# Issuing the load of token tile 1 from ScalarE's DMA queue instead of second in SyncE's

## The chip, the cores and the metric

The kernel runs on one core of a Trainium2 chip. The metric is the device time of one execution in microseconds (us). "Tile n" is the block of 128 tokens with number n. Times inside an execution count from the start of the profiled span.

## The reference, cut to what matters

```python
xn = layernorm(x)                        # x: 2048 tokens x 1024, bf16
s  = attention(xn, wqkv, wo)             # 32 heads of 32
g  = silu(mlp(layernorm(xn), w1, b1, w2, b2))
return x + s * g
```

Nothing of the attention can start before tiles are loaded and normalised, so the first loads of x and the first statistics are the kernel's start-up.

## The kernel before

The program is written as a list of operations. A small scheduler records each one with its engine and what it reads and writes, works out the semaphore waits, and uses an estimated clock to decide in which order filler work is queued. The loads come first, all on SyncE's queue:

```python
def load_x(tb):
    op("sync", lambda e: e.dma_start(xst[:, tb * D:(tb + 1) * D], x2[tb * 128:(tb + 1) * 128, :]),
       w=[("xst", tb)], dma=f"x{tb % 8}", c=256)
# [...]
load_x(0)
load_x(1)
load_x(2)
load_wq(0, (1,))     # 512 KB of weights
load_x(3)
load_wq(0, (0,))
load_x(4)
load_x(5)
load_wq(0, (2,))
for tb in range(6, NT):
    load_x(tb)
# [...]
```

VectorE takes the statistics of tile 0, ScalarE those of tile 1 (two passes over the tile), and GpSimd does the power for the reciprocal standard deviation:

```python
def norm_pair(p):
    if p == 0:
        stat(0)            # VectorE, L324, L328
        rstd(0, 1)         # VectorE L338, GpSimd L340
        stat_scalar(1)     # ScalarE L715, L716, L717, then GpSimd L718, L719
        xnorm(0)           # VectorE L359
        bn_half(2, 0)      # VectorE L324
        xnorm(1)           # VectorE L359: needs tile 1's factor
        bn_half(2, 1)
        bn_merge(2)
        # [...]
```

TensorE transposes the normalised tiles (L386), makes K and Q (L689) and V (L705), and then scores (L872). ScalarE's exp (L884) and TensorE's matmuls fill the rest of the run.

The softmax here doesn't subtract the row's maximum and nothing guards it: scores larger than these inputs give would overflow.

## Time and profile before

| Kernel before | us |
|---|---|
| device time, median of 3 runs | 1090.31 (1090.11 to 1090.38) |
| span of the profiled run | 1088.8 |
| tile 0 lets VectorE start | 3.35 |
| tile 1 lets ScalarE start | 4.03 |
| normalisation of tile 1 (VectorE) starts | 7.41 |
| first exp starts | 14.79 |

The profile's instruction rows read: start, duration, engine, line and operation, output<-input, shapes, count; in brackets the idle time before and who ended it. A load's own row is only its issue (SPq, ACTq). When it landed is seen from the row of the engine that waited for it, or from the DMA row of the chain. The rows of the start-up are shown in the prediction.

### The profile page before, as it was taken

Reading aid. Unit: us, or ns where it says so; the run is one execution under the profiler, and the core shown is the slowest. Engines: PE = TensorE matmul, PEld = TensorE weight load, DVE = VectorE, ACT = ScalarE, POOL = GpSimd, SP = SyncE. Lnnn points to the kernel's source line nnn. Section 1 sums busy time; section 2 is a strip of 40 time slices with the busy share of each in tenths; the row PEclk is TensorE's granted clock in tenths of the full one; section 3 lists DMA queues with packets and bytes.
Section 4 is the critical chain, followed back from the end, with each engine's and each line's share of the span. In section 5 each row is a group of like instructions: output and inputs, shape, how many; then the busy total and the mean of one; then the engine's idle time right before and its main releaser. Section 6 shows DMA issues by size and latency. Waiting matters only on the chain.

```text
span 1088.8 us, 61842 instructions
## 1 busy us (share of the span) xinstructions
PE 1078.1 (99%) x29167; PEld 701.4 (64%) x29167; DVE 627.6 (58%) x1396; ACT 1043.9 (96%) x1197; POOL 22.4 (2%) x69
## 2 busy tenths in 40 slices
PE   9999999999999999999999999999999999999998
PEld 6766666666666666666666666666666666666665
DVE  8487843477732576642377743378733387635556
ACT  7899998999999999999999999999999999999993
POOL 4400000000000000000000000000000000000000
PEclk9999999999999999999999999999999999999999
DMA  7944365413464214355333274423253343684534
GB/s 242 185 127 139 119 177 138 125 52 110 119 154 123 68 59 128 101 104 148 90 100 100 73 155 124 120 81 109 81 135 115 91 123 106 192 206 105 109 92 123
DMA packets 209336, 131.92 MB, mean 121 GB/s; under 512 B 52538, under 2 KB 200250, under 8 KB 209082
## 3 DMA queue, kind: packets, MB, share of 16 engines
q1 hardware_dynamic: 209082, 127.97, 43.4%
q8 instruction: 228, 3.74, 1.5%
q14 instruction: 26, 0.21, 0.1%
HBM read 104.87 MB, written 12.06 MB: 107 GB/s over the span
## 4 chain that ended last, share of the span: by engine, by line
PE 57%; ACT 41%; DVE 1%; DMA 0%; issue 0%; POOL 0%; SPq 0%
ACT P L884 37%; PE ps L395 34%; PE ps L872 9%; PE ps L901 6%; PE ps L904 6%; ACT u L565 4%; PE ps L705 1%; PE ps L689 1%; DVE stats L324 0%; DMA OT<-in_A_x_dram 0%; ACT thz L609 0%; DVE wq L669 0%; DVE hT L359 0%; ACT hT L716 0%; DVE wq L671 0%
## 5 line engine op out<-in xcount | busy, mean ns | idle before, releaser
L884 ACT ACTIVATE P<-ps 128x1024 bf16<-128x1024 f32 x1024 | 968.9, 1084 | 10.3 <-PE ps L872 5.4
L901 PE MATMUL ps<-P,VP 128*32 128x256 bf16 x4096 | 257.0, 273 | 0.5 <-issue 0.5
L904 PE MATMUL ps<-P,ones 128*32 128x256 bf16 x4096 | 256.8, 273 | 0.0
L395 PE MATMUL ps<-hT,war 128*32 128x352 bf16 (+1 forms) x5376 | 225.8, 309 | 0.1
L395 PE MATMUL ps<-yTc,war 128*32 128x352 bf16 (+1 forms) x5376 | 225.3, 309 | 0.0
L872 PE MATMUL ps<-QT,KT 32*128 32x256 bf16 x4096 | 203.7, 273 | 3.4 <-issue 0.6
L395 PEld LDWEIGHTS ps<-hT,war 128*32 128x32 bf16 x5376 | 128.0, 96 | 74.4 <-issue 25.8
L395 PEld LDWEIGHTS ps<-yTc,war 128*32 128x32 bf16 x5376 | 127.3, 96 | 74.2 <-DVE xb L548 18.9
L872 PEld LDWEIGHTS ps<-QT,KT 32*128 32x128 bf16 x4096 | 60.8, 92 | 115.6 <-issue 61.9
L605 DVE TENSOR_SCALAR zh<-ps,b2h 128x352 f32<-128x352 f32 (+1 forms) x48 | 27.5, 572 | 183.4 <-PE ps L395 183.4
L548 DVE TENSOR_SCALAR xb<-ps,b1T 128x352 f32<-128x352 f32 (+1 forms) x168 | 96.2, 573 | 48.7 <-PE ps L395 44.2
L571 DVE SCALAR_TENSOR_TENSOR hT<-u,xb 128x352 bf16<-128x352 f32 (+1 forms) x168 | 84.4, 509 | 68.3 <-ACT u L565 68.2
L901 PEld LDWEIGHTS ps<-P,VP 128*32 128x32 bf16 x4096 | 109.8, 97 | 21.3 <-issue 2.1
L904 PEld LDWEIGHTS ps<-P,ones 128*32 128x32 bf16 x4096 | 109.7, 97 | 18.6
L395 PE MATMUL ps<-xnT,wq 128*32 128x352 bf16 (+1 forms) x2688 | 112.7, 309 | 0.0
L395 PEld LDWEIGHTS ps<-xnT,wq 128*32 128x32 bf16 x2688 | 63.7, 96 | 37.2 <-DVE xb L548 8.9
L558 DVE SCALAR_TENSOR_TENSOR u<-u,xb 128x352 f32<-128x352 f32 (+1 forms) x168 | 82.5, 509 | 1.9
L554 DVE TENSOR_TENSOR u<-xb 128x352 f32<-128x352 f32 (+1 forms) x168 | 82.5, 507 | 0.7
L565 ACT ACTIVATE u<-u 128x704 f32<-128x704 f32 (+1 forms) x84 | 71.8, 859 | 0.0
L395 PE MATMUL ps<-xnT,OT 128*32 128x352 bf16 (+2 forms) x1568 | 62.9, 306 | 0.2 <-DVE wq L669 0.2
L395 PE MATMUL ps<-wq,xnT 128*32 128x256 bf16 x1536 | 50.8, 274 | 0.0
L395 PEld LDWEIGHTS ps<-xnT,OT 128*32 128x32 bf16 x1568 | 37.9, 96 | 19.7 <-DVE wq L669 7.7
(61 smaller groups left out, 477.3 us busy)
## 6 DMA issues: line engine op xcount, KB each, us to landing
war<-in_B_w_dram SPq DMA_DIRECT2D x336, 256.0 KB, 3.4
wq<-in_A_wqkv_dram SPq DMA_DIRECT2D x36, 128.0 KB, 2.3
OT<-in_A_x_dram SPq DMA_DIRECT2D x16, 256.0 KB, 5.7
xnT<-in_A_x_dram SPq DMA_DIRECT2D x16, 256.0 KB, 2.9
out_dram<-wq SPq DMA_DIRECT2D x15, 256.0 KB, 2.0
y_scratch<-OT SPq DMA_DIRECT2D x14, 256.0 KB, 2.4
gT_scratch<-gst SPq DMA_DIRECT2D x32, 88.0 KB, 3.3
xnT<-in_A_wo_dram SPq DMA_DIRECT2D x8, 256.0 KB, 4.0
```

The costliest lines, as they stand in the source:

```text
L395: ins = e.matmul(outs(j), lhsT=lhs(j), rhs=rhs, start=start, stop=stop, tile_position=(0, 32 * j), skip_group_check=True)
L548: x0 = op("vector", lambda e: e.tensor_scalar(xb[:, 0:n], bank(bk, 0, n), b1T[:, f:f + 1], None, op0=ALU.add), r=[("b", bk), "b1"], w=[kx] ...
L554: x = op("vector", lambda e: e.tensor_tensor(ub[:, 0:n], xb[:, 0:n], xb[:, 0:n], op=ALU.mult), r=[kx], w=[ku], c=151 + 1.042 * n)
L558: x = op("vector", lambda e: e.scalar_tensor_tensor(ub[:, 0:n], ub[:, 0:n], 1.0 / 0.044715, xb[:, 0:n], op0=ALU.add, op1=ALU.mult), r=[kx, ...
L565: x = op("scalar", lambda e: e.activation(ut[:, :, 0:n], ut[:, :, 0:n], ACT.Tanh, scale=0.7978845608028654 * 0.044715), r=kus, w=kus, c=48 ...
L571: op("vector", lambda e: e.scalar_tensor_tensor(hT[:, fq, 0:n], ut[:, i, 0:n], 1.0, xq[:, 0:n], op0=ALU.add, op1=ALU.mult), r=[kus[i], kq] ...
L605: x0 = op("vector", lambda e: e.tensor_scalar(zh[:, 0:n], bank(bk, 0, n), 0.25, b2h[:, nb:nb + 1], op0=ALU.mult, op1=ALU.add), r=[("b", bk ...
L689: ins = e.matmul(bank(bk, off, off + w), lhsT=wq[:, which, dc, 0:128], rhs=xnT[:, dc, t0 + lo:t0 + lo + w], start=dc == 0, stop=dc == DC - ...
L872: ins = e.matmul(bank(bks[j], kh * 256, (kh + 1) * 256), lhsT=KT[i2][32 * j:32 * j + 32, k0:k0 + 128], rhs=QT[i2][32 * j:32 * j + 32, qb * ...
L884: op("scalar", lambda e, p=p, sl=sl: e.activation(pb[:, 2 * p:2 * p + 2, :, :].rearrange("p a b q -> p (a b q)"), ps[:, sl * 1024:(sl + 1) ...
L901: e.matmul(bankq(ACC, j, 0, QW), lhsT=VP[vp][:, kb, vo + 32 * j:vo + 32 * j + 32], rhs=pb[:, j, kh, :], start=first, stop=False, tile_posi ...
L904: ins = e.matmul(bankq(ACC, j, QW, 2 * QW), lhsT=ones[:, 0:32], rhs=pb[:, j, kh, :], start=False, stop=last, tile_position=(0, 32 * j), sk ...
```

## The change

The intent is to save one issue slot on SyncE: tile 1 is issued at the same moment as tile 0, by an engine that waits for it anyway.

```diff
         def load_x(tb):
-            op("sync", lambda e: e.dma_start(xst[:, tb * D:(tb + 1) * D], x2[tb * 128:(tb + 1) * 128, :]),
+            op("scalar" if tb == 1 else "sync", lambda e: e.dma_start(xst[:, tb * D:(tb + 1) * D], x2[tb * 128:(tb + 1) * 128, :]),
                w=[("xst", tb)], dma=f"x{tb % 8}", c=256)
```

## The prediction

> **What bounds the kernel now.** I read the page from the top: busy shares, the chain that ended last, then the chain in order of time for the first 18 us, because the change touches one of the first instructions. After that came the instructions of VectorE and ScalarE in order of time, and the windows by stage, which give the DMA rate.
>
> The page's busy shares and its chain by engine:
>
> ```profile
> PE 1078.1 (99%) x29167; PEld 701.4 (64%) x29167; DVE 627.6 (58%) x1396; ACT 1043.9 (96%) x1197; POOL 22.4 (2%) x69
> PE 57%; ACT 41%; DVE 1%; DMA 0%; issue 0%; POOL 0%; SPq 0%
> ```
>
> TensorE and ScalarE share the bound. No wait on a DMA shows in the body at all. Only the prologue can feel this change, and it is small: VectorE and DMA together are about 1% of the chain.
>
> The same chain in order of time, at the start (start, duration, what):
>
> ```profile
> 0.72 0.39 SPq L275
> 1.11 0.06 issue
> 1.17 2.83 DMA OT<-in_A_x_dram
> 4.00 0.02 issue
> 4.03 1.16 ACT hT L715 x2
> 5.18 0.03 issue
> 5.21 1.24 ACT hT L716 x2
> 6.45 0.10 ACT mv L717
> 6.55 0.19 POOL lnp L718
> 6.73 0.07 issue
> 6.81 0.58 POOL lnp L719
> 7.38 0.03 issue
> 7.41 0.55 DVE hT L359
> ```
>
> This is exactly the transfer that is moved. Tile 1 is issued at 1.17, one issue slot behind tile 0, and lands at 4.00. ScalarE's statistics of it, GpSimd's power and VectorE's normalisation at 7.41 hang on it. From there the chain goes down VectorE's queue to the transposes of tiles 4 and 5 at 16.53, after which TensorE runs almost without a gap. So whatever this landing gains or loses can reach the end one for one, and hardly more.
>
> How much room stands beside it, from VectorE's and then ScalarE's instructions in order of time (in brackets: idle time before, and who ended it):
>
> ```profile
> 3.35 1.29 DVE L324 BATCH_NORM_STATS2 stats<-OT 128x6 f32<-128x512 bf16 x2 [1.99 <-DMA OT<-in_A_x_dram]
> 6.21 0.69 DVE L324 BATCH_NORM_STATS2 stats<-OT 128x6 f32<-128x512 bf16 x1
> 7.41 0.55 DVE L359 TENSOR_SCALAR hT<-OT,mv,lnp 128x1024 bf16<-128x1024 bf16 x1 [0.51 <-POOL lnp L719]
> ...
> 0.72 1.28 ACT L715 ACT_TABLE_LOAD   x1 [0.72 <-PEq L1044]
> 4.03 1.06 ACT L715 ACTIVATE hT<-OT 128x1024 bf16<-128x1024 bf16 x1 [2.02 <-DMA OT<-in_A_x_dram]
> ```
>
> Tile 0 lets VectorE start at 3.35. VectorE's own queue, fed by tile 0, arrives at 6.90 (6.21 + 0.69) and then stands idle 0.51 us until tile 1's factor comes. So tile 0's side has 0.51 us of slack against tile 1's side; a gain on tile 1 is worth at most 0.51, and only if tile 0 does not get later.
>
> The DMA rate in stages (last two columns: share of the DMA engines, GB/s):
>
> ```profile
> 2.50:2.75 0.25, 0.25 (x2) 0.11 (x1) 0.00 (x0) 0.00 (x0) 0.00 (x0) 1.00 1.02 385
> 2.75:3.00 0.25, 0.25 (x2) 0.04 (x1) 0.00 (x0) 0.00 (x0) 0.00 (x0) 1.00 1.10 385
> 12.00:14.00 2.00, 2.00 (x24) 1.81 (x22) 1.97 (x5) 1.57 (x2) 1.52 (x5) 1.00 1.05 405
> ```
>
> While tiles 0 and 1 arrive the engines already move 385 GB/s, near the best they reach anywhere (405).
>
> **What the Trainium skill says.** "DMA: Bandwidth & Descriptors", section "Issuing engines are not separate DMA queues": transfers started by different engines run on the same 16 DMA engines and interleave, and a second issuer only saves issue time. The trace agrees so far as it can: tiles 0 and 1, issued 0.45 us apart (0.72 and 1.17), land 0.67 us apart (the shortest issue-to-landing time of these loads is 2.6 us, 0.72 + 2.6 = 3.3, against 4.00), and 262,144 B in 0.67 us is 391 GB/s, the full rate. Tile 1 follows tile 0 at the pace of the bytes, not of the issues. Same page, "Queues, rings and completion order": an engine takes turns between the queues that have work, a packet at a time. No run here shows this yet; before, all data is on one queue. "Perfetto Trace Analysis", section "DMA Instruction — HWDGE (DVE, Sync)": descriptor generation is one shared block that an issuing sequencer locks, so two issues at 0.72 may not run side by side; also not shown yet. "ScalarE: Activation LUTs", "What ACT_TABLE_LOAD costs": 1283 ns for the load; the trace has 1.28 us.
>
> **The change part by part.**
>
> 1. SyncE loses one issue: tile 2 and everything after it is issued about 0.45 to 0.47 us earlier (0.39 us of issue plus the gap). That is worth nothing later on: from 6 us to 16 us the queue is the limit (359 to 405 GB/s in the windows), and the bytes are the same. Tile 2 is not needed until 6.21 and tile 3 until 8.72.
>
> 2. ScalarE gains one issue as its first instruction, at 0.72. I estimate it at SyncE's 0.39 us, or about twice that, 0.8 us, if it waits for the shared block. The table load belongs to the first ACTIVATE (it carries that line), so it should follow the issue: it ends at 2.4 to 2.8 instead of 2.0. ScalarE then waits for tile 1 anyway until about 4. Cost on the path: 0, since there are 2.02 us of idle time there.
>
> 3. Tile 1's issue moves from 1.17 to 0.72 (or about 1.1 behind the lock). If issue were what it waits for, this would give 0.45 us. It is not: tile 0 holds the engines until its own bytes are through. At 391 GB/s the two tiles together take 1.34 us of all 16 engines, whichever goes first, so the later of the two still lands at about 4.0.
>
> 4. The order can become a mixture. If the engines alternate between the two queues, tile 0 is slowed by up to 0.67 us (3.33 to 4.0). 0.51 of it is slack, so 0.16 us reaches the normalisation of tile 1. If ScalarE's issue is the later one by 0.39 us, tile 0 has 0.28 us left and becomes 0.28 us later, which is inside the slack; but then tile 1 shares the engines with tile 2, which is now right behind tile 0, and finishes its second half at half rate: it has had 0.28 us worth by then, and the 0.39 us that are left take 0.78, so tile 1 lands 0.39 us later, 4.4.
>
> 5. The program's build-time clock decides the order of all other work. It charges each load 870 ns of transfer against 480 ns of issue, so in it the transfers set all landing times and they stay what they were. ScalarE's clock starts at 480 ns instead of 0, long before its first input. I expect the same instruction order on every other engine, so no change in the body.
>
> Sum: 0 (steps 1, 2, 5) plus step 3 and 4, from 0 to +0.4 us, and I take +0.1 us: 1090.31 + 0.1 = 1090.4 us.
>
> **The rivals.** *Issue-bound*: tile 1 really lands 0.45 us earlier. For it: before 2.5 us the engines are not full (106 GB/s from 1.5 to 2.0, 197 and 229 in the next two quarters), and a second queue could fill those holes. Against it: the 0.67 us between the landings. Were tile 1 at 3.55, VectorE's idle 0.51 would shrink to 0.06; TensorE's idle time before the transposes of tile 3 is 0.37, so about 0.4 us would come out at the end: 1089.9. *Mixture*: both tiles late, as in step 4: 1090.5 to 1090.7. *Table load first*: were the table load put ahead of the issue, tile 1 would be issued at 2.0 instead of 1.17, and everything on SyncE's queue would be ahead of it or alternate with it; it would land 0.8 us later or more: 1091.1 or above. Against it: the load's line is the first ACTIVATE's. *A cold second queue*: ScalarE's first transfer may need longer to start than the 1.03 us after which I see the first data of tile 0 (issued 0.72, moving at 1.75); nothing before shows it; each 0.1 us costs 0.1.
>
> **Range and chances.** The three runs before lie within 0.27 us. The outcomes above lie between -0.4 and +0.8; I give about 20% to a gain of 0.2 to 0.5, 45% to a change within 0.15, 30% to a loss of 0.15 to 0.6, and 5% to more. That makes 1089.9 to 1091.0 for 8 in 10. Two per cent is 21.8 us; all the waiting in the prologue that depends on this load is under 4 us, so within 2% is all but sure: faster 0.005, same 0.99, slower 0.005.
>
> **What would show it.** In the changed kernel: ScalarE's issue stands at 0.72 ahead of the table load (step 2); its first ACTIVATE starts at 4.0 to 4.4 (steps 3 and 4; at 3.6 the issue-bound rival is right; after 4.7 the table load or a cold queue); VectorE's first statistics at 3.35 to 4.0 (step 4); the normalisation of tile 1 at 7.4 to 7.8; TensorE's transposes of tiles 4 and 5 move from 16.53 by the same amount; from 6 us on the DMA rate is as before (step 1). It would be wrong if the order of instructions in the body changed, or if the shift at 16.53 did not reach the end one for one.

## The result

The changed kernel took 1090.68 us, median of 5 runs (1090.19 to 1091.53). The kernel before, with two more runs, had a median of 1090.11 (1088.63 to 1090.38). The ratio was 1.0007, 95% interval 0.9993 to 1.002. The single comparison does not tell a loss from nothing. The trace of the start-up does.

The page of the changed kernel, chain by engine (in the kernel before it was PE 57% and ACT 41%; VectorE and DMA are about 1% in both):

```profile
PE 55%; ACT 44%; DVE 1%; DMA 0%; issue 0%; POOL 0%
```

The chain of the changed kernel in order of time, at the start (start, duration, what):

```profile
0.73 3.93 DMA OT<-in_A_x_dram
4.66 0.02 issue
4.68 1.16 ACT hT L715 x2
...
8.18 0.55 DVE hT L359
```

In this profile the chain is the same up to the normalisation of tile 1, link by link, but tile 1 now takes 3.93 us from issue to landing instead of 2.83. It was issued 0.44 us earlier and landed 0.66 us later. The normalisation of tile 1 moved from 7.41 to 8.18.

Instructions of the changed kernel in order of time (ScalarE's issue, its table load, VectorE's and ScalarE's first work, the work of VectorE on tile 2):

```profile
0.73 0.40 ACTq L275 DMA_DIRECT2D OT<-in_A_x_dram  x1
1.16 1.28 ACT L715 ACT_TABLE_LOAD   x1 [1.16 <-PEq L1044]
4.50 1.29 DVE L324 BATCH_NORM_STATS2 stats<-OT 128x6 f32<-128x512 bf16 x2 [3.15 <-DMA OT<-in_A_x_dram]
4.68 1.06 ACT L715 ACTIVATE hT<-OT 128x1024 bf16<-128x1024 bf16 x1 [2.24 <-DMA OT<-in_A_x_dram]
7.37 0.69 DVE L324 BATCH_NORM_STATS2 stats<-OT 128x6 f32<-128x512 bf16 x1
```

Tile 0, which was not touched, is the bigger loser: VectorE starts on it at 4.50 instead of 3.35. The two tiles now land within 0.2 us of each other. VectorE's own queue gets to 8.06 (7.37 + 0.69), so nearly all of the 0.51 us in which it stood idle before tile 1's normalisation is gone. ScalarE's issue cost nothing by itself: 0.40 us, and its table load was done at 2.44, long before the tile came.

The windows by stage, two stages of each kernel (last column GB/s). Before:

```profile
1.75:2.50 0.75, 0.75 (x3) 0.30 (x2) 0.00 (x0) 0.26 (x1) 0.00 (x0) 1.00 0.87 210
2.50:3.50 1.00, 1.00 (x4) 0.31 (x3) 0.15 (x1) 0.00 (x0) 0.00 (x0) 1.00 0.97 356
```

After:

```profile
1.75:2.50 0.75, 0.75 (x3) 0.30 (x2) 0.00 (x0) 0.69 (x1) 0.00 (x0) 1.00 0.60 167
2.50:3.50 1.00, 1.00 (x4) 0.32 (x3) 0.00 (x0) 0.00 (x0) 0.00 (x0) 1.00 0.99 326
```

The engines did not move more with two queues feeding them, but a little less: 0.75 x 167 + 326 = 451 KB by 3.5 us, against 0.75 x 210 + 356 = 514 KB. At 391 GB/s the difference is 0.16 us. It is not a chance of this pair: from 1.5 to 3.5 us the three profiles of the kernel before moved 258, 241 and 245 GB/s and those of the changed kernel 225, 223 and 200, which in the mean is again 0.16 us.

One more row of the changed kernel matters, TensorE's weight loads for the first V:

```profile
13.31 1.64 PEld L705 LDWEIGHTS ps<-wq,xnT 128*128 128x128 bf16 x16 [0.21 <-DMA wq<-in_A_wqkv_dram]
```

Here V waited for the third block of weights as well. In the kernel before it started at 12.35 without that wait. Whether the second queue did that too is one of the questions below.

### The profile page after: what moved, and what is told of

Same layout as the page of the kernel before. It is cut to its first block, busy times and chain, and to the rows that moved or that the text cites. A ratio compares the mean times of both kernels' runs of the same rounds, so it can differ in the third digit from the quotient of the medians.

```text
span 1089.1 us, 61842 instructions
## 1 busy us (share of the span) xinstructions
PE 1077.0 (99%) x29167; PEld 701.0 (64%) x29167; DVE 627.2 (58%) x1396; ACT 1043.8 (96%) x1197; POOL 22.6 (2%) x69
## 3 DMA queue, kind: packets, MB, share of 16 engines
q8 instruction: 228, 3.74, 1.5%
## 4 chain that ended last, share of the span: by engine, by line
PE 55%; ACT 44%; DVE 1%; DMA 0%; issue 0%; POOL 0%
ACT P L884 40%; PE ps L395 32%; PE ps L872 9%; PE ps L901 6%; PE ps L904 5%; ACT u L565 4%; PE ps L705 1%; PE ps L689 1%; DMA OT<-in_A_x_dram 0%; ACT thz L609 0%; DVE stats L324 0%; PE ps L386 0%; DVE wq L669 0%; ACT hT L716 0%; DVE wq L671 0%
```

## The experiments

**Theory (mixture).** Two queues that start together are served in turn by the same DMA engines, so both tiles are done only when both are through. **Rivals.** *Chance*: one of the 16 parts of a load was slow in the one profile. *The moved load itself*: ScalarE's queue or its issue is slow to start. *A second queue as such* costs something, whatever it carries. *The table load* belongs ahead of the issue and delays it.

All kernels gave correct results. The instruction order on TensorE, VectorE, ScalarE and GpSimd of each edited kernel was compared with that of the kernel before; apart from the added and moved instructions it is the same. The repeats labelled again carry one comment line on top, so their line numbers are one higher. The diffs below are shortened (...); in hold_tile2, tile2_on_act, both_on_act, act_after_table and offset_only they are against the changed kernel, in the others against the kernel before.

| Kernel | VectorE starts (tile 0) | ScalarE starts (tile 1) | tile 1 normalised from | first exp | ratio to before, 95% interval |
|---|---|---|---|---|---|
| before | 3.35 | 4.03 | 7.41 | 14.79 | |
| again_before | 3.53 | 4.19 | 7.57 | 14.97 | 0.9999 (0.9987 to 1.0012) |
| third_before | 3.43 | 4.16 | 7.54 | 15.06 | 1.0001 (0.9988 to 1.0013) |
| after | 4.50 | 4.68 | 8.18 | 15.77 | 1.0007 (0.9993 to 1.002) |
| again_after | 4.98 | 4.80 | 8.44 | 15.80 | 1.0009 (0.9995 to 1.0022) |
| third_after | 4.75 | 4.57 | 8.21 | 15.57 | 1.0006 (0.9992 to 1.0019) |
| hold_tile2 | 4.18 | 4.34 | 7.86 | 16.64 | 1.0013 (1.0001 to 1.0026) |
| swap_on_sync | 4.12 | 3.44 | 7.59 | 14.95 | 1.0005 (0.9993 to 1.0018) |
| tile2_on_act | 4.53 | 5.28 | 8.67 | 16.04 | 1.0009 (0.9996 to 1.0023) |
| bias_on_act | 3.53 | 4.16 | 7.62 | 15.56 | 1.0005 (0.9991 to 1.0019) |
| both_on_act | 3.37 | 3.97 | 7.43 | 17.42 | 1.0016 (1.0001 to 1.0031) |
| split_tile0 | 2.98, second half 4.42 | 3.93 | 7.51 | 15.84 | 1.0017 (1.0004 to 1.003) |
| act_after_table | 3.74 | 4.36 | 7.82 | 15.19 | 1.0008 (0.9995 to 1.0022) |
| offset_only | 3.86 | 4.51 | 7.89 | 15.26 | 1.0007 (0.9995 to 1.002) |

The whole times cannot carry a verdict on a few tenths of a microsecond: single runs of the kernel before lay between 1088.55 and 1092.01. Only the intervals of hold_tile2, both_on_act and split_tile0 lie wholly above 1. The start-up in the profiles can, because the normalisation of tile 1 and the first exp repeat within 0.3 us.

### again_before and third_before: the kernel before, unchanged

> The kernel before, unchanged, to see how much of its prologue and of its whole time repeats. Mixture theory (the two queues share the DMA engines, so the second queue is what made tiles 0 and 1 late): tile 0 lands at 3.3 to 3.4, tile 1 at 3.9 to 4.1, the normalisation of tile 1 starts at 7.3 to 7.5, the transposes of tile 4 at 16.4 to 16.7, as in the first profile. Chance theory (one of the 16 DMA engines was slow in the one profile of the changed kernel, whatever the queues): such a slow engine turns up in this kernel's second profile about as often, and tile 0 may land at 4 or later. Time against the kernel before: ratio 1.000, and a spread of single runs of 0.5 us or more, since the first two sets of runs of the same program lay at 1088.6 to 1090.4.

> The kernel before a third time. What is open: in several profiles one of the 16 parts of a load lands 1 to 2 us after the others (in the first profile of the changed kernel the third part of the first weights landed at 13.3, and V had to wait for it), and it is not clear whether the second queue causes that or chance. Mixture theory, with the late part as chance: tile 0 at 3.3 to 3.6, tile 1 at 3.9 to 4.2, normalisation of tile 1 at 7.3 to 7.6; the last part of the third weights may land anywhere from 11.9 to 13.3. Second queue as the cause of the late part: here it lands at 11.9 to 12.5 again, as in the first two. Whole time: ratio to the kernel before 0.999 to 1.001.

Measured: tile 0 lets VectorE start at 3.53 and 3.43, tile 1 ScalarE at 4.19 and 4.16, the normalisation of tile 1 starts at 7.57 and 7.54. The start-up of the first profile repeats to 0.2 us. No profile of this kernel shows tile 0 after 3.6, so chance alone does not explain 4.50. The body, on the other hand, does not repeat. The longest single waits of TensorE's weight loads for the scores, between 340 and 560 us (total us, times, longest us), in the first profile:

```profile
PEld ps L872 <- issue: 10.7, 48, 0.8
```

and in third_before:

```profile
PEld ps L872 <- issue: 10.3, 49, 0.2
```

The first profile has single stalls of 0.7 to 0.8 us, with nothing visible that TensorE waited for; the third has none there. From 345 to 644 us the first profile loses 1.65 us on the third. Stalls of 0.3 to 1.5 us turn up at other places in other profiles, of both kernels and of the edited ones. Stalls of this size help to spread the whole time; what causes them is open. The last of the 16 parts of the third weights, which V needs, landed at 12.48 and 12.56 here and at 11.92 in the first profile. At 12.56 it is a little past the 12.5 that the second queue as the cause allowed.

### again_after and third_after: the changed kernel, unchanged

> The changed kernel, unchanged. Mixture theory: tile 0 lands at 4.2 to 4.6 and tile 1 at 4.4 to 4.8 again, the normalisation of tile 1 starts 0.6 to 0.9 us later than before, the first exp 0.8 to 1.0 us later, and the whole is 0.3 to 0.9 us slower (ratio 1.0003 to 1.0008). Chance theory: tile 0 lands at 3.4 to 4.0 and tile 1 at about 4.0, the normalisation of tile 1 at 7.4 to 7.6, and the whole is within 0.2 us of the kernel before.

> The changed kernel a third time. Mixture theory: tile 0 at 4.2 to 5.0, tile 1 at 4.5 to 4.9, normalisation of tile 1 at 8.1 to 8.5, first exp 0.8 to 1.0 us later than in the kernel before; ratio 1.0003 to 1.0012. If the second queue also causes the late part: the last part of the third weights lands after 12.7; as chance: anywhere from 11.9.

Measured: both land late again, in all three profiles. Over the three pairs of profiles the means are (differences taken before rounding): tile 0 from 3.44 to 4.74 (+1.31), tile 1 from 4.13 to 4.68 (+0.56), the normalisation of tile 1 from 7.51 to 8.28 (+0.77), the first exp from 14.94 to 15.71 (+0.77). The chance rival falls. The last part of the third weights landed at 12.73 and 12.48, which the second queue as its cause (after 12.7) does not fit in third_after. In again_after the wait has changed sides; VectorE in order of time:

```profile
7.84 0.69 DVE L325 BATCH_NORM_STATS2 stats<-OT 128x6 f32<-128x512 bf16 x1
8.44 0.53 DVE L360 TENSOR_SCALAR hT<-OT,mv,lnp 128x1024 bf16<-128x1024 bf16 x1
```

There is no bracket before the normalisation: VectorE comes straight from its own queue, which tile 0 had held up, and no longer waits for tile 1's factor. The same is so in third_after. In these two profiles the chain that ended last starts at tile 0's landing (4.95 and 4.73) and runs down VectorE's queue; only in the first profile does it start at tile 1's. So the change mostly turned a wait for tile 1 into a late tile 0.

The end gets about all of it. At the 100th exp, at 134 us, the three profiles of the changed kernel are on average 0.78 us behind the three of the kernel before (mean offsets to third_before of +0.72 and -0.06). After that the body's stalls blur it in a single profile. Pooled, 15 runs of the changed kernel have a mean of 1090.74 us and 42 runs of the kernel before one of 1089.96. The difference is 0.78 us with a standard error of 0.20 (from standard deviations of 0.54 and 0.90). The runs come from several chips, so this supports the trace rather than standing alone.

### tile2_on_act: another tile on ScalarE's queue

```diff
-            op("scalar" if tb == 1 else "sync", ...
+            op("scalar" if tb == 2 else "sync", ...
```

> Tile 1 stays second on SyncE; tile 2, which nobody needs before 6.2 us, goes to ScalarE's queue instead. Mixture theory: it takes every second turn of the engines from the start, so tile 0 lands at 4.0 to 4.9 and tile 1 even later than with the change, at 4.5 to 5.5, although tile 1 was not touched; the normalisation of tile 1 starts 0.7 to 1.5 us later than before and the first exp 0.8 us later or more. Rival, a property of the moved load itself (its issue, its own start-up on ScalarE's queue): tiles 0 and 1 land at 3.3 to 3.5 and 4.0 to 4.2 as before, and the prologue is as before.

Measured, VectorE and ScalarE in order of time:

```profile
4.53 1.29 DVE L324 BATCH_NORM_STATS2 stats<-OT 128x6 f32<-128x512 bf16 x2 [3.17 <-DMA OT<-in_A_x_dram]
5.28 1.06 ACT L715 ACTIVATE hT<-OT 128x1024 bf16<-128x1024 bf16 x1 [2.84 <-DMA OT<-in_A_x_dram]
8.67 0.55 DVE L359 TENSOR_SCALAR hT<-OT,mv,lnp 128x1024 bf16<-128x1024 bf16 x1 [0.59 <-POOL lnp L719]
```

Tiles 0 and 1 stand where they stood before the change, on the same queue in the same order, and are 1.1 to 1.2 us later than before's means (3.44 and 4.13), because a tile that nobody needed yet shared the engines with them. The mixture theory holds. The rival that the moved load itself is slow falls.

### both_on_act: ScalarE's queue by itself

```diff
-            op("scalar" if tb == 1 else "sync", ...
+            xo[tb] = op("scalar" if tb < 2 else "sync", ...
-               w=[("xst", tb)], dma=f"x{tb % 8}", c=256)
+               w=[("xst", tb)], dma=f"x{tb % 8}", c=256, after=[xo[0]] if tb == 2 else ())
```

> Tiles 0 and 1 both from ScalarE's queue, one behind the other, and SyncE starts with tile 2 once tile 0 has landed: ScalarE's queue alone, nothing mixed until then. Mixture theory: tile 0 lands at 3.3 to 3.5 and tile 1 at 4.0 to 4.3, as from SyncE; in between the landings 0.65 to 0.75. Rival, ScalarE's queue is slower to start (0.36 us in the first profile of the changed kernel): tile 0 at 3.7 or later, tile 1 at 4.4 or later. The rest comes later than before in either case (tile 2 after 5.5), so the whole is slower by 0.5 to 1.5 us in the prologue.

Measured, VectorE and ScalarE in order of time:

```profile
3.37 1.29 DVE L324 BATCH_NORM_STATS2 stats<-OT 128x6 f32<-128x512 bf16 x2 [2.01 <-DMA OT<-in_A_x_dram]
3.97 1.06 ACT L715 ACTIVATE hT<-OT 128x1024 bf16<-128x1024 bf16 x1 [1.08 <-DMA OT<-in_A_x_dram]
```

Alone, ScalarE's queue is as quick as SyncE's: 3.37 and 3.97, 0.60 apart. No cold queue. The first exp came 2.5 us later than in before's three profiles, since everything behind was held back on purpose; the expectation of 0.5 to 1.5 us for that was too low.

### bias_on_act: a second queue with almost nothing in it

```diff
-            op("sync", lambda e: e.dma_start(brow[0:FB, :], ...
+            op("scalar", lambda e: e.dma_start(brow[0:FB, :], ...
-            op("sync", lambda e: e.dma_start(brow[FB:FB + DC, :], ...
+            op("scalar", lambda e: e.dma_start(brow[FB:FB + DC, :], ...
```

> All tiles stay on SyncE; only the two small bias loads (9 KB together) are issued from ScalarE at the start. The second queue is opened, but has next to nothing to share. Mixture theory: tile 0 lands at 3.3 to 3.6 and tile 1 at 4.0 to 4.3, the normalisation of tile 1 at 7.3 to 7.6. Rival, opening a second queue costs by itself (the engines' start, or the shared descriptor generator): tile 0 lands after 3.8 and tile 1 after 4.4.

Measured, VectorE's normalisation of tile 1 and TensorE's first V:

```profile
7.62 0.55 DVE L359 TENSOR_SCALAR hT<-OT,mv,lnp 128x1024 bf16<-128x1024 bf16 x1 [0.34 <-POOL lnp L719]
13.11 1.92 PE L705 MATMUL ps<-wq,xnT 128*128 128x256 bf16 x16 [0.39 <-DMA wq<-in_A_wqkv_dram]
```

The tiles came as before (3.53 and 4.16), so an open second queue is not what delays them; its bytes are. But the first exp still came at 15.56, because V waited for the weights, the same wait as in the first profile of the changed kernel. In the trace's semaphore records the 16 parts of that load landed between 11.3 and 13.1. It is a second way for the start-up to get late, and it appears without a tile on ScalarE's queue.

### hold_tile2: tiles 0 and 1 alone on the engines

```diff
-               w=[("xst", tb)], dma=f"x{tb % 8}", c=256)
+               w=[("xst", tb)], dma=f"x{tb % 8}", c=256, after=[xo[0]] if tb == 2 else ())
```

(with tile 1 on ScalarE, and `xo[tb]` keeping each load)

> The changed kernel, but SyncE holds tile 2 and all behind it back until tile 0 has landed, so tiles 0 and 1 have the DMA engines to themselves. Mixture theory with tile 2 as the third sharer: tile 1 lands at about 4.0 and tile 0 at 3.7 to 4.0 (two tiles need 1.34 us of engine time from 1.75, plus 0.6 to 0.9 until the semaphore), the normalisation of tile 1 at 7.4 to 7.6; but tile 2 is issued only at about 4, lands after 6, and the weights come later, which costs TensorE. Rival, slow start of ScalarE's queue (its first data came 0.36 us after SyncE's): tile 1 lands at 4.3 or later even with nothing behind it.

Measured, VectorE in order of time:

```profile
4.18 1.29 DVE L324 BATCH_NORM_STATS2 stats<-OT 128x6 f32<-128x512 bf16 x2 [2.82 <-DMA OT<-in_A_x_dram]
```

Tile 1 came at 4.34. Without a third load behind them both are earlier than in the changed kernel (4.50 to 4.98 and 4.57 to 4.80), but not at the 3.7 to 4.0 and 4.0 that I expected of the mixture alone: tile 0 is 0.74 us later than before's mean of 3.44, tile 1 0.21 later. Sharing between the two tiles gives more than half of tile 0's loss. What lies behind them gives the rest or part of it; one profile cannot fix its share. The weights came later, as expected, and the first exp at 16.64.

### swap_on_sync: tile 1 first, on one queue

```diff
-        load_x(0)
         load_x(1)
+        load_x(0)
```

> The kernel before with tile 1 issued first and tile 0 second, both on SyncE: undoes the second queue, keeps the idea that tile 1 should come earlier. One queue in order: tile 1 lands at 3.3, tile 0 at 4.0. VectorE's work on tile 0 then starts at 4.0, the normalisation of tile 1 is held by VectorE's own queue at about 7.55, 0.15 us later than before; the transposes of tile 4 at 16.6 to 16.8. If tile 1's landing alone set the prologue, the normalisation of tile 1 would start at 6.75 instead. Time: within 0.3 us of the kernel before.

Measured, VectorE in order of time:

```profile
7.59 0.53 DVE L359 TENSOR_SCALAR hT<-OT,mv,lnp 128x1024 bf16<-128x1024 bf16 x1
```

One queue keeps order here: tile 1 came at 3.44 and tile 0 at 4.12. The normalisation of tile 1 then waited for VectorE's own queue (no bracket), at 7.59, 0.08 after before's mean. The slack of about 0.5 us on tile 0's side is real, and giving tile 1 the first place uses it up for nothing.

### split_tile0: a version that might have beaten both

```diff
-        load_x(0)
-        load_x(1)
+        load_x(0, 0, 512); load_x(1)
+        load_x(0, 512, D)
```

(load_x takes a range of columns; the statistics of tile 0 wait for each half by itself)

> A version that might beat both: one queue, in the order first half of tile 0's columns, tile 1, second half of tile 0. The mixture is chosen by order instead of by two queues. In a queue served in order: first half lands at about 3.0, tile 1 at 3.7, second half at 4.0. VectorE's first statistics start at 3.0, its second at 4.0, done at 4.7 as before; tile 1's factor comes 0.3 us earlier, the normalisation of tile 1 at 7.0 to 7.2, the first exp 0.2 to 0.4 us earlier than before. If half rows (1 KB pieces instead of 2 KB) move more slowly, the second half lands after 4.2 and the gain is gone. Whole time: 0.3 us less, below what the runs resolve (single runs of the kernel before spread over 3 us).

Measured, VectorE in order of time:

```profile
2.98 0.69 DVE L324 BATCH_NORM_STATS2 stats<-OT 128x6 f32<-128x512 bf16 x1 [1.62 <-DMA OT<-in_A_x_dram]
4.42 0.69 DVE L324 BATCH_NORM_STATS2 stats<-OT 128x6 f32<-128x512 bf16 x1 [0.75 <-DMA OT<-in_A_x_dram]
```

A miss. The first half came at 2.98 as expected, but tile 1 at 3.93 instead of 3.7 and the second half at 4.42 instead of 4.0. The normalisation of tile 1 starts at 7.51, the mean of before, so nothing was gained there, and V again waited for the weights (its first matmul at 13.39, 0.41 us of idle time ended by that load). No version here beats the kernel before.

### act_after_table: my rival of the table load

```diff
-        load_x(0)
-        load_x(1)
+        load_x(0); op("vector", lambda e: e.memset(lnp[:, 3, 0:1], 0.0), w=["pre"], c=100.0)
+        op("scalar", lambda e: e.activation(lnp[:, 3, 1:2], lnp[:, 3, 0:1], ACT.Tanh), ...); load_x(1)
```

> The changed kernel with a tiny activation ahead of ScalarE's issue, so that the table load comes first and tile 1 is issued at about 2.2 to 2.4: my rival of the table load, made real. Mixture theory: tile 0 has the engines almost to itself and lands at 3.3 to 3.7, as before; tile 1 then takes every second turn beside tile 2 and the first weights, needs two times 0.67 us from about 3.3, and lands at 5.0 to 5.6; the normalisation of tile 1 at 8.4 to 9.0, the first exp 1.0 to 1.6 us later than before. If instead the early issue is what delayed tile 1 (both queues starting cold at once), tile 1 lands within 2 us of its issue, at 4.4 or earlier.

Measured, ScalarE in order of time:

```profile
0.72 1.28 ACT L299 ACT_TABLE_LOAD   x1 [0.72 <-PEq L1044]
...
0.89 0.38 ACTq L275 DMA_DIRECT2D OT<-in_A_x_dram  x1
```

The run did not do what it was built for. The issue stood behind the table load and the activation in ScalarE's queue, and went out at 0.89 while the table load ran until 2.00. The issue does not wait for the work ahead of it to finish, only for the semaphore that VectorE's fill set, so the table load was never a rival. The 0.17 us that the fill cost had an effect of its own: tile 0 at 3.74 and tile 1 at 4.36, 0.62 apart, so no longer in step. Both came earlier than in all three profiles of the changed kernel, although tile 1 was issued later. That asked for the next run.

### offset_only: ScalarE's issue 0.16 us behind SyncE's

```diff
-        load_x(0)
-        load_x(1)
+        load_x(0); pre = op("vector", lambda e: e.memset(lnp[:, 3, 0:1], 0.0), w=["pre"], c=100.0)
+        load_x(1, [pre])
```

> The changed kernel, but ScalarE's issue waits for a one-column fill by VectorE, so that it starts about 0.15 us after SyncE's; the table load stays behind the issue. In the run with the tiny activation the issue came at 0.89 (it did not wait for the table load, as I had thought), and the engines then served tile 0, tile 1 and tile 2 one after the other. If the 0.17 us of offset did that (two issues that start together have their rows dealt out in turn, two that start apart do not): tile 0 lands at 3.3 to 3.8, tile 1 at 4.0 to 4.4, 0.6 to 0.7 apart, and the normalisation of tile 1 starts at 7.4 to 7.9. If the order was chance, or came from the activation or the table load: the tiles alternate again, both land between 4.2 and 5.0 and within 0.2 of each other, and the normalisation of tile 1 starts at 8.1 to 8.5. Whole time within what the runs resolve in either case.

Measured, in order of time:

```profile
0.88 0.38 ACTq L275 DMA_DIRECT2D OT<-in_A_x_dram  x1
...
3.86 1.29 DVE L324 BATCH_NORM_STATS2 stats<-OT 128x6 f32<-128x512 bf16 x2 [2.50 <-DMA OT<-in_A_x_dram]
7.89 0.55 DVE L359 TENSOR_SCALAR hT<-OT,mv,lnp 128x1024 bf16<-128x1024 bf16 x1 [0.48 <-POOL lnp L719]
```

Tile 1 came at 4.51, 0.65 after tile 0 and just outside the 4.0 to 4.4 that I gave. The two tiles are served one after the other again, without an activation and with the table load in its usual place. The offset did it. The trace's DMA records say the same: each of the 16 parts of a load ends with a 4-byte write. With both issues within 0.01 us of each other (changed kernel, three profiles) the earliest such write of tile 0 stands at 3.36 to 3.50, beside the earliest of tile 1 at 3.36 to 3.49; the rows were dealt out in turn. With 0.16 to 0.17 us between the issues, tile 0's stand at 2.62 to 3.49 and tile 1's at 3.42 to 4.14. That the engines take rows in the order in which the issues hand them over is my inference; it fits, and no run shows the mechanism.

Even so both tiles are about 0.2 to 0.4 us later than before in these two runs (the normalisation at 7.82 and 7.89, against a mean of 7.51). So rows dealt out in turn are not the whole cause: 0.31 to 0.38 of the changed kernel's 0.77 is left without them. tile2_on_act has such a remainder too: sharing alone would put its tiles at about 4.13 and 4.80 (my estimate: tile 0 at tile 1's old time, tile 1 one tile's 0.67 later), and they came at 4.53 and 5.28. Part of it is the rate. From 1.5 to 3.5 us the engines moved 200 to 225 GB/s in all six profiles with a tile on each queue and more loads right behind (the changed kernel's three, tile2_on_act and these two), against 241 to 261 in the three of the kernel before, swap_on_sync, bias_on_act, both_on_act and hold_tile2. For this run, 220 against before's mean of 248 is worth 0.14 us at 391 GB/s. One queue is no guarantee: split_tile0, with half rows, moved 215. Why the rate is lower, and the rest, stay unexplained.

## Why the prediction was right or wrong, point by point

The measured 1090.68 lies in the range of 1089.9 to 1091.0, and within 2% was right. That the number fits is partly luck: two errors cancel (see the sum). The working beneath it was right in most of its structure and wrong in two sizes, and with them in the path.

- **The path.** Right in that the start-up's shift reaches the end about one for one: +0.77 at the normalisation, +0.77 at the first exp, +0.78 at 134 us, and +0.78 in the pooled runs. Right only in one profile of three in that tile 1's landing sets it: in the other two the chain comes from tile 0 over VectorE's own queue. That no wait on a DMA shows in the body was not quite so either: two weight loads of TensorE waited for one after 16 us (at 24.64 and 29.15), 0.5 us together, too little to matter here.
- **Step 1, SyncE's earlier issues are worth nothing.** Right. Tile 2 was issued at 1.17 instead of 1.64, and neither the tiles' statistics nor the first V came earlier in any profile of the changed kernel.
- **Step 2, ScalarE's issue is free.** Right, at the lower figure: 0.39 to 0.40 us in all three profiles, with no sign in the issue's row of waiting for the shared block that the Trainium skill describes in "Perfetto Trace Analysis", section "DMA Instruction — HWDGE (DVE, Sync)", though both engines issued within 0.01 us. In the DMA records one queue's first row came 0.10 to 0.36 us after the other's; whether the block does that is open.
- **Step 3, the later of the two tiles still lands at about 4.0.** This step failed. The later of the two came at 4.68, 4.98 and 4.75, mean 4.80, against a mean of 4.13 in the three profiles of before: 0.68 us for which the sum had 0. Two parts of it show. The engines moved less while both queues started (about 0.16 us), and the 16 parts spread out: in the DMA records the earliest closing write of tile 1 hardly moved (means 3.47 before, 3.44 after), the latest went from 3.76 to 4.27. Why some parts lag is open; holding tile 2 back brought the later of the two to 4.34.
- **Step 4, the mixture.** Right in kind, wrong in size for tile 0: I gave it at most +0.67, it lost 1.31, because what the pair lost in step 3 comes on top of the sharing (0.69, from 3.44 to tile 1's old 4.13). So of the slack of 0.51 next to nothing is left. The expected half rate beside tile 2 is not what delays tile 1 by itself: with both issues offset, and tile 2 right behind, the tiles kept their order.
- **Step 5, the same instruction order.** Right, checked on every engine. (In the traces at most 48 of TensorE's 29167 matmul records stand in another order inside short groups; between unchanged copies up to 24 do.)
- **The sum.** +0.1 us was too small; the start-up lost 0.77, and the pooled runs 0.78 with a standard error of 0.20. A loss of that size was in the class to which I gave 5%. The number still fell in the range because the base was off the other way: the three runs gave 1090.31, the 42 runs have a mean of 1089.96. With the true shift on my base, 1090.31 + 0.77 = 1091.08, it would have been just outside.
- **The signs.** ScalarE's issue stood ahead of the table load, as I said, and the transposes of tiles 4 and 5 moved from 16.53 to 17.31 in the first profile. But tile 1 came at 4.57 to 4.80 and not at 4.0 to 4.4, tile 0 at 4.50 to 4.98 and not at 3.35 to 4.0, the normalisation at 8.18 to 8.44 and not at 7.4 to 7.8. Read by my list, a tile 1 after 4.7 (4.80 in again_after) would have pointed to the table load or a cold queue, and it was neither.
- **The rivals.** Issue-bound fell: tile 1 came later, not at 3.6. The cold queue fell (both_on_act), the table load fell (act_after_table).
- **The noise.** I took the spread of the kernel before as 0.27 us from three runs. With 42 runs its standard deviation is 0.90. The range held for the median by more luck than its width admits.

Left open: why the last parts of the third weights' load land 1 to 2 us after its first in some profiles (13.27 against 11.36 in the first of the changed kernel, but 11.92 against 11.27 in the first of the kernel before). It made V wait in the first profile of the changed kernel, in hold_tile2, bias_on_act and split_tile0. It is not tied to a tile on ScalarE's queue (bias_on_act, split_tile0), it did not make V wait in again_after or third_after, and in three profiles of the kernel before it never reached V.

## What to carry to other kernels

When two transfers land at a distance that equals one transfer's bytes at the full rate, as here (0.67 us), expect the second to wait for bytes and not for its issue, and a second queue to take from the first. Order on one queue is a tool: here it gave the transfer that is needed first all of the engines, while two queues that started at the same moment finished both tiles later than the second of them had come before (4.74 and 4.68 against 4.13). To judge a change of a few tenths of a microsecond in a run of a millisecond, compare the start-up in several profiles; the whole times of the same program spread by more than 3 us.

## What the Trainium skill lacked or had wrong

- "DMA: Bandwidth & Descriptors", section "Issuing engines are not separate DMA queues", says that a second issuer only saves issue time. It does not say that it can cost: the two transfers interleave, and here the load that was not moved lost 1.31 us and the moved one 0.56.
- Same page, "Queues, rings and completion order", has an engine take turns between queues a packet at a time, a packet being typically 9 to 17 descriptors. A part of a tile here is 8 rows and a closing write. If such a part is one packet, whole tiles in turn would fit the page. With both issues within 0.01 us the tiles finished in step (earliest closing writes at 3.36 to 3.50 for both); with 0.16 to 0.17 us between them they came one after the other, 0.62 to 0.65 us apart. The page says nothing of the dependence on when the issues start.
